# First slot of a fused attention and expert kernel: v's buffer 192 B longer, GpSimd's weight splits placed anew, routing with three small operations fewer, the ranks' product later on TensorE

## The chip, the cores and the metric

The kernel runs on one core of one Trainium2 chip. The metric is the time of one execution on the device in microseconds; less is better. The engines have short names in the profile: PE is TensorE (PEld its weight load), DVE is VectorE, ACT is ScalarE, POOL is GpSimd, SP is SyncE, which here only issues DMAs. A line such as L258 is a line of the kernel.

## The reference

Inputs are q, k and v for 8 batches, 8 heads, 576 tokens and head size 64, a modality id for each of the 4608 tokens, a gate, biases, eight experts' weights w1 (512x1024) and w2 (1024x512), and a last two-layer network with 512x2048 and 2048x512 weights.

```python
# linear attention: softmax of q over the head size, of k over the tokens
q_s = softmax(q, axis=-1); k_s = softmax(k, axis=2)
x = q_s @ (k_s^T @ v)                        # per batch and head, then [4608, 512]
# one expert for each token
logits = x @ w_gate + modality_bias[modality_id]
e_idx = argmax(logits)
gate_w = exp(l - max)[e_idx] / (sum(exp(l - max)) + 1e-9)
for e in range(8):
    mask = e_idx == e
    out[mask] = gate_w[mask] * (relu(x[mask] @ w1[e]) @ w2[e])
# last network
h = out @ w_in
result = max(0.01 * h, h) @ w_out
```

## The kernel before

The work stands in one program order, written out by hand, and each engine runs its own instructions in that order, waiting for what it needs.

**Attention** goes over four pairs of batches, i = 0 to 3. Each pair has nine chunks of 128 tokens, c = 0 to 8; (i, c) names a chunk here, and 9i + c is its place in time. The function `attention` makes a list of steps, each with a time in units of a chunk, and sorts it; the sorted list is the program order. For each chunk, `trans` transposes q on TensorE and ScalarE takes its exponent; `xmm` makes the product with the k-v matrix on TensorE and ScalarE copies the sums (ri) and the gate's logits (lr); `evac` on VectorE takes the reciprocal (L256), scales the product out of PSUM (L258), and SP stores it to xd. Two PSUM buffers hold the product of a chunk, so `xmm` of chunk n waits for `evac` of chunk n - 2. For the next pair, `kmax`, `kexp`, `kv`, `krec`, `kvn`, `kvT` and `kg` make the k-v matrix between them. `qmax` (VectorE, L219) and `qsub` (GpSimd, L223, 128x1536) take the maximum off q, a third of a pair at a time.

**Routing** (`phase_r`) is done for five groups of chunks: 0 to 8, 9 to 17, 18 to 26, 27 to 32 and 33 to 35; a route is named here by its first chunk. Its steps r0 to r16 are small VectorE instructions on all tokens of the group: logits, maximum, a one-hot choice oh, the counts of each expert (r8, tot), r9 (casts of the counts so far, tacc, and of tot to bf16, L326 and L327), r9t (tacc plus tot, L340), rm (the ranks' product on TensorE, with a triangle of ones, L332 to L336), r10 (the sum of exponents), r11 (plus 1e-9, L346), r12 to r15 (the row of every token, with a scan at L353) and r16 (that row as an integer, L362). Then `scat` on GpSimd writes each chunk's token numbers and weights to their rows of the table `region` by an indirect DMA (L365). A scatter may be `paced`: a copy of one element (L377) ahead of it waits for a given chunk's ri.

**The first slot.** Tokens are computed in slots of 512 of one expert. The first slot takes the expert with the most tokens of route 0, so that it can begin before the other routes are known. `First` chooses it. Its steps stand in the same list (`prepare`): `loads_to` loads chunks of w1 and w2 into a ring of five, `place1`, `place2` and `place3` reuse attention's k, v and q buffers for the split weights and operands, `idload` reads the tokens' numbers from `region` (SP, L624), `xids` casts them (L628), `xgather` fetches their rows of xd (GpSimd, four indirect DMAs, L633), `xgate1` scales them on ScalarE, and `xprep` transposes them. A float32 operand is split into a high part, rounded by a ScalarE cast (L510), and the rest, by a subtraction (L511) on VectorE or, where `eng` says so, GpSimd:

```python
def split(nc, hi, lo, src, eng=None):
    nc.scalar.copy(out=hi, in_=src)
    (eng or nc.vector).tensor_tensor(out=lo, in0=src, in1=hi.bitcast(F32), op=ALU.subtract)
```

`wsplit(s, which, c, eng, most)` does it for a quarter c of w1 or w2 of slot s. `slot0` is the first slot's first pass, x times w1: eight groups f of 12 matmuls (`pass1`, L659), each with a relu on ScalarE and a rest (`low`, L662) on VectorE. Steps of the sorted list that come after time 36.04 are run by `tail(f)` between its groups. `slot_tables` makes the table of all later slots there, in parts, with a small product on TensorE (L457). `slot0b` is the second pass, times w2 (`pass2`, L670), and gathers for slot 1. Then come the later slots (`slot`), up to 16 of them, with the same lines, the last network's weights being converted between their steps, and then the last network (`Hidden`, L934; `last_product`, L1093).

Of the kernel before, what the change touches and what calls it, by code (L numbers as in the profile page):

```python
# [99 lines left out]
def attention(ctx, pools, tc, cst, a, region, xd, first):  # L100
# [16 lines left out]
    tacc = cst["tacc"]  # L117
    kt, vt, qt = {}, {}, {}
    lr = one.tile([128, NPAIR * NC, 4, 16], F32, name="lr")
    ri = one.tile([128, NPAIR * NC, 4, 2], F32, name="ri")  # L120

    def load_kv(i, hp):
        if hp == 0:
            kt[i] = kp.tile([128, 4, 2 * S], F32, tag="k", name=f"k{i}")
            vt[i] = kp.tile([128, 4, 2, 5, 130], F32, tag="v", name=f"v{i}")
# [148 lines left out]
    def phase_r(c0, c1):  # L274
# [3 lines left out]
        t, rp = {}, {}  # L278

        def r0():  # L280
            t["lp"] = sp.tile([128, NC, 8, NE], F32, tag="lp", name="lp", bufs=1)[:, 0:n]
            for x in ("lg", "ex", "w"):
                t[x] = sp.tile([128, NC, NE], F32, tag=x, name=x)[:, 0:n]
# [5 lines left out]
            t["tot"] = sp.tile([128, NE], F32, tag="tot", name="tot")  # L289
            t["tb"] = sp.tile([128, 2, NE], BF16, tag="tb", name="tb")  # L290
# [19 lines left out]
        def rx():  # L310
            nc.scalar.activation(out=t["ex"], in_=t["lg"], func=AF.Exp)
# [10 lines left out]
        def r8():  # L322
            nc.vector.tensor_reduce(out=t["tot"], in_=t["oh"][:, :, 1:n + 1], axis=AX.X, op=ALU.add)

        def r9():
            nc.vector.tensor_copy(out=t["tb"][:, 1], in_=tacc)  # L326
            nc.vector.tensor_copy(out=t["tb"][:, 0], in_=t["tot"])  # L327

        def rm():
            bank = ps_k.tile([128, 3 * NE], F32, tag="kv", name="rp")  # L330
            rp[0] = bank[:, 0:NE]
            nc.tensor.matmul(bank[0:2 * NE, NE:2 * NE], lhsT=t["tb"].rearrange("p a e -> p (a e)"), rhs=trib[:, 0:NE], start=True, stop=True)  # L332
            nc.tensor.matmul(rp[0], lhsT=trib, rhs=t["tb"][:, 0], start=True, stop=False)
            nc.tensor.matmul(rp[0], lhsT=onesb, rhs=t["tb"][:, 1], start=False, stop=True)
            if c0 == 0:
                nc.tensor.matmul(bank[:, 2 * NE:3 * NE], lhsT=onesb, rhs=t["tb"][:, 0], start=True, stop=True)  # L336
                first.counts = bank[:, 2 * NE:3 * NE]

        def r9t():
            nc.vector.tensor_tensor(out=tacc, in0=tacc, in1=t["tot"], op=ALU.add)  # L340
# [3 lines left out]

        def r11():
            nc.vector.tensor_scalar(out=t["gs"], in0=t["gs"], scalar1=1e-9, scalar2=None, op0=ALU.add)  # L346
# [899 lines left out]
```

## Time and profile before

| what | value |
|---|---|
| runs | 1395.70, 1391.75 and 1393.58 us; median 1393.58 us |
| the profiled execution | 1389.55 us, of which the span of instructions is 1387.8 us |
| TensorE busy | 1319.7 us (95%), 9185 matmuls |
| VectorE, ScalarE, GpSimd busy | 1039.1, 584.5 and 333.2 us |
| granted TensorE clock, mean | 0.979 |

The runs are timings without a profile; all rows below are of the profiled execution, in us from the start of its span. TensorE's share is an average over stages: the attention stage ends at about 177 us, the first slot's passes go to about 235, the later slots to about 638 and the last network to the end.

### The profile page before, as it was taken

The page shows a single profiled execution, that of the slowest core. Times are in us where ns is not written, and L with a number is a line of the kernel's source. Part 1 is how long each engine was busy: PE and PEld are TensorE (multiplying, and loading weights), DVE is VectorE, ACT ScalarE, POOL GpSimd, SP SyncE. Part 2 cuts the span into 40 slices and gives each one's busy share as a digit, 9 for nine tenths or more (in the row PEclk, how much of TensorE's full clock was granted, in tenths as well). Part 3 has the DMA queues.
Part 4 walks back from the last instruction along what each step waited for, and adds up shares of the span by engine and source line. Part 5 has one row for each costly group of instructions (what it writes and reads, how often), then busy time and mean ns, then how long its engine had stood idle before and what let it go on. Part 6 is the DMA issues. An engine that isn't in the chain of part 4 may idle for free.

```text
span 1387.8 us, 23465 instructions
## 1 busy us (share of the span) xinstructions
PE 1319.7 (95%) x9185; PEld 1224.5 (88%) x9185; DVE 1039.1 (75%) x1398; ACT 584.5 (42%) x914; POOL 333.2 (24%) x285
## 2 busy tenths in 40 slices
PE   6997789999999999998999999999989999999998
PEld 6986667888878877888899999999979999999998
DVE  5789775778787777647678777778677877787775
ACT  4556424544555455454333233332233333333332
POOL 2227661111001100111343433333411110111011
PEclk9999799999999999999999999999999999999999
DMA  9874317779788887877823333323893434343430
GB/s 368 344 277 161 126 43 268 249 250 307 242 287 263 285 277 227 278 257 290 313 96 152 122 140 135 122 95 150 321 403 126 153 122 134 126 140 127 120 117 31
DMA packets 146444, 279.06 MB, mean 201 GB/s; under 512 B 18192, under 2 KB 69904, under 8 KB 145424
## 3 DMA queue, kind: packets, MB, share of 16 engines
q1 hardware_dynamic: 121536, 207.93, 44.4%
q10 hardware_dynamic: 17232, 48.48, 8.8%
q0 software_dynamic: 7552, 21.02, 4.4%
q8 instruction: 75, 1.23, 0.4%
q14 instruction: 49, 0.40, 0.1%
HBM read 181.07 MB, written 96.32 MB: 200 GB/s over the span
## 4 chain that ended last, share of the span: by engine, by line
PE 29%; DVE 11%; issue 7%; POOL 3%; DMA 2%; ACT 1%; POOLq 0%; SPq 0%; DVEq 0%; ACTq 0%
PE yp L1093 24%; PE hp L934 6%; POOL s L974 3%; DVE ht L947 2%; DVE ht L983 1%; DVE ht L980 1%; DVE s L971 1%; DVE ht L967 1%; DVE x L511 1%; DVE s L969 1%; POOL s L975 1%; DMA wi<-wid 1%; DMA hd<-ht 1%; DMA wo<-wod 1%; DVE xl L511 0%
## 5 line engine op out<-in xcount | busy, mean ns | idle before, releaser
L934 PE MATMUL hp<-xh,wi 128*128 128x256 f32 x1152 | 213.1, 281 | 4.7 <-DVE ht L983 2.3
L659 PE MATMUL hp<-xq,xk 128*128 128x512 f32 (+1 forms) x640 | 194.8, 388 | 0.9 <-issue 0.6
L1093 PE MATMUL yp<-wi,x 128*128 128x256 f32 x1152 | 191.4, 283 | 0.0
L934 PEld LDWEIGHTS hp<-xh,wi 128*128 128x128 f32 x1152 | 179.5, 188 | 7.5 <-DVE ht L983 3.5
L1093 PE MATMUL yp<-wi,wi 128*128 128x256 f32 x1200 | 178.2, 283 | 0.3 <-DVE wi L511 0.3
L934 PE MATMUL hp<-x,wi 128*128 128x256 f32 x1296 | 164.1, 286 | 5.5 <-ACTq L844 3.6
L934 PEld LDWEIGHTS hp<-x,wi 128*128 128x128 f32 x1296 | 160.5, 194 | 6.0 <-ACTq L844 3.8
L1093 PEld LDWEIGHTS yp<-wi,wi 128*128 128x128 f32 x1200 | 163.5, 192 | 0.6 <-DVE wi L511 0.6
L1093 PEld LDWEIGHTS yp<-wi,x 128*128 128x128 f32 x1152 | 161.9, 192 | 0.1
L934 PE MATMUL hp<-xl,wi 128*128 128x256 f32 x576 | 160.7, 279 | 0.0
L670 PE MATMUL yp<-xq,xk 128*128 128x512 f32 (+1 forms) x400 | 143.5, 388 | 0.6 <-DVE xq L662 0.6
L659 PEld LDWEIGHTS hp<-xq,xk 128*128 128x128 f32 x640 | 119.1, 190 | 27.8 <-issue 1.0
L633 POOL DMA_INDIRECT xg<-xd,idi x44 | 52.6, 1195 | 369.1 <-ACT xq L661 167.6
L511 DVE TENSOR_TENSOR xv<-st,xk 128x1024 fp32r<-128x1024 f32 x78 | 95.4, 1223 | 51.9 <-ACT xk L510 51.5
L659 PE MATMUL hp<-xq,xv 128*128 128x512 f32 (+1 forms) x320 | 123.7, 387 | 0.0
L670 PE MATMUL yp<-xq,xv 128*128 128x512 f32 (+1 forms) x320 | 123.1, 385 | 0.0
L1115 POOL DMA_INDIRECT out<-yo,idx x36 | 47.3, 1314 | 315.2 <-DVE idx L1109 294.3
L934 PEld LDWEIGHTS hp<-xl,wi 128*128 128x128 f32 x576 | 108.0, 187 | 0.0
L947 DVE SCALAR_TENSOR_TENSOR ht<-ht 128x1024 f32<-128x1024 f32 x72 | 104.9, 1457 | 2.5
L974 POOL TENSOR_TENSOR s<-s,s 128x512 f32<-128x512 f32 x36 | 48.6, 1351 | 211.0 <-DVE s L971 161.7
L510 ACT CAST xk<-st 128x1024 fp32r<-128x1024 f32 x84 | 87.6, 1044 | 13.9 <-ACT y L676 8.8
L661 ACT ACTIVATE xq<-hp 128x512 fp32r<-128x512 f32 (+1 forms) x80 | 46.1, 576 | 105.2 <-PE hp L659 100.2
(219 smaller groups left out, 2431.8 us busy)
## 6 DMA issues: line engine op xcount, KB each, us to landing
st<-in_w SPq DMA_DIRECT2D x88, 512.0 KB, 6.5
hd<-ht ACTq DMA_DIRECT2D x72, 512.0 KB, 3.0
xt<-hd SPq DMA_DIRECT2D x18, 1024.0 KB, 5.5
hr<-hd SPq DMA_DIRECT2D x18, 1024.0 KB, 5.3
wi<-wid SPq DMA_DIRECT2D x28, 512.0 KB, 9.2
wi<-wod SPq DMA_DIRECT2D x6, 2048.0 KB, 12.0
v<-in_v SPq DMA_DIRECT2D x16, 650.0 KB, 10.1
k<-in_k SPq DMA_DIRECT2D x16, 576.0 KB, 9.7
```

The lines of the kernel that those rows point to most:

```text
L510: nc.scalar.copy(out=hi, in_=src)
L511: (eng or nc.vector).tensor_tensor(out=lo, in0=src, in1=hi.bitcast(F32), op=ALU.subtract)
L633: nc.gpsimd.indirect_dma_start(out=xg[:, t], out_offset=None, in_=xd[0:n], in_offset=bass.IndirectOffsetOnAxis(ap=idis[s % 2][:, t:t + 1], ...
L659: nc.tensor.matmul(hp[:, rows], lhsT=w[:, k, 128 * f:128 * f + 128], rhs=x[:, k, rows], start=(n == 0), stop=(n == 11))
L661: nc.scalar.activation(out=hh[:, f, rows], in_=hp[:, rows], func=AF.Relu)
L670: nc.tensor.matmul(yp[:, rows], lhsT=w[:, f, 128 * d:128 * d + 128], rhs=h[:, rows], start=(n == 0), stop=(n == 23))
L934: self.nc.tensor.matmul(bank[:, g], lhsT=w[:, h, k, 128 * g:128 * g + 128], rhs=x[:, k], start=(n == 0), stop=(n == 5))
L947: V.scalar_tensor_tensor(out=c, in0=c, scalar=0.01, in1=c, op0=ALU.mult, op1=ALU.max)
L967: V.tensor_tensor(out=h[:, 0, 0], in0=bank, in1=s[1], op=ALU.add)
L974: G.tensor_tensor(out=s[6], in0=s[6], in1=s[5], op=ALU.add)
L1093: nc.tensor.matmul(bank, lhsT=x[:, k], rhs=w[i][:, h, k], start=(c == 0), stop=(c == 23))
L1115: ins = nc.gpsimd.indirect_dma_start(out=out, out_offset=bass.IndirectOffsetOnAxis(ap=idi[s % 2][:, t:t + 1], axis=0), in_=y[:, t], in_off ...
```

## The change

In the kernel after, v's buffer has 5248 elements of each partition in place of 5200, of which the first 5200 are used as before. Routing keeps the counts in one bf16 table `acc` with a place for each route, so that r9's two casts fall away: r8 writes its counts there, r9t adds them up there, and rm reads them there. The exponents have a ninth column that holds 1e-9, so that r10's sum has it and r11 falls away; r15 writes integers, so that r16 falls away. Scatters of routes 0, 9, 27 and 33 have other times, r12 to r15 of route 9 come later, and the ranks' products of routes 27 and 33 too have other times (the last one is run by `tail` of group 2 instead of group 1, that of 27 just ahead of the first pass). In `prepare`, the id load, the ids' cast and the gather come earlier, three of the four w1 splits are GpSimd's and come earlier, the fourth is VectorE's, and `xprep` is in two steps. In `slot0`, all four w2 splits are VectorE's, at other groups, the rests are computed later, and the tables are made at groups 2 and 3.

```diff
+VROW = 5248
...
+    acc, exs = cst["acc"], one.tile([128, 2, NC, NE + 1], F32, name="exs")
+    nc.gpsimd.memset(exs[:, :, :, NE], 1e-9)
...
     def load_kv(i, hp):
...
-            vt[i] = kp.tile([128, 4, 2, 5, 130], F32, tag="v", name=f"v{i}")
+            vt[i] = kp.tile([128, VROW], F32, tag="v", name=f"v{i}")[:, 0:5200].rearrange("p (h j c e) -> p h j c e", h=4, j=2, c=5)
...
+        tot, old, new = acc[:, u, 0], acc[:, u, 1], acc[:, u + 1, 1]
...
         def r0():
...
-            t["tot"] = sp.tile([128, NE], F32, tag="tot", name="tot")
-            t["tb"] = sp.tile([128, 2, NE], BF16, tag="tb", name="tb")
+            t["ex"] = exs[:, u % 2, 0:n]
...
         def rx():
-            nc.scalar.activation(out=t["ex"], in_=t["lg"], func=AF.Exp)
+            nc.scalar.activation(out=t["ex"][:, :, 0:NE], in_=t["lg"], func=AF.Exp)
...
         def r8():
-            nc.vector.tensor_reduce(out=t["tot"], in_=t["oh"][:, :, 1:n + 1], axis=AX.X, op=ALU.add)
-        def r9():
-            nc.vector.tensor_copy(out=t["tb"][:, 1], in_=tacc)
-            nc.vector.tensor_copy(out=t["tb"][:, 0], in_=t["tot"])
+                nc.vector.tensor_reduce(out=tot, in_=t["oh"][:, :, 1:n + 1], axis=AX.X, op=ALU.add)
...
         def rm():
...
-            nc.tensor.matmul(bank[0:2 * NE, NE:2 * NE], lhsT=t["tb"].rearrange("p a e -> p (a e)"), rhs=trib[:, 0:NE], start=True, stop=True)
-            nc.tensor.matmul(rp[0], lhsT=trib, rhs=t["tb"][:, 0], start=True, stop=False)
-            nc.tensor.matmul(rp[0], lhsT=onesb, rhs=t["tb"][:, 1], start=False, stop=True)
+            nc.tensor.matmul(bank[0:2 * NE, NE:2 * NE], lhsT=acc[:, u].rearrange("p a e -> p (a e)"), rhs=trib[:, 0:NE], start=True, stop=True)
+            nc.tensor.matmul(rp[0], lhsT=trib, rhs=tot, start=True, stop=False)
+            nc.tensor.matmul(rp[0], lhsT=onesb, rhs=old, start=False, stop=True)
...
-                nc.tensor.matmul(bank[:, 2 * NE:3 * NE], lhsT=onesb, rhs=t["tb"][:, 0], start=True, stop=True)
+                nc.tensor.matmul(bank[:, 2 * NE:3 * NE], lhsT=onesb, rhs=tot, start=True, stop=True)
...
         def r9t():
-            nc.vector.tensor_tensor(out=tacc, in0=tacc, in1=t["tot"], op=ALU.add)
+            nc.vector.tensor_tensor(out=new, in0=old, in1=tot, op=ALU.add)
...
         def r10():
...
-        def r11():
-            nc.vector.tensor_scalar(out=t["gs"], in0=t["gs"], scalar1=1e-9, scalar2=None, op0=ALU.add)
...
         def r15():
-            nc.vector.tensor_reduce(out=t["mx"], in_=t["st"][:, :, 0:n].rearrange("p e c -> p c e"), axis=AX.X, op=ALU.add)
-        def r16():
-            nc.vector.tensor_copy(out=t["ix"][:, 0:n], in_=t["mx"])
+                nc.vector.tensor_reduce(out=t["ix"][:, 0:n], in_=t["st"][:, :, 0:n].rearrange("p e c -> p c e"), axis=AX.X, op=ALU.add)
...
-    slow = dict(r0=1.15, r1=2.5, r2=3.5, rx=4.4, r5=4.5, r8=5.6, rm=6.55, r10=6.6, r12=7.6, r13=7.61, r16=8.5)
-    mid = dict(r0=0.2, r1=0.9, r2=1.2, rx=2.1, r5=2.15, r8=2.6, rm=3.3, r10=3.4, r12=4.1, r16=4.6)
-    fast = dict(r0=0.2, r2=0.6, rx=1.45, r5=1.15, rm=3.05)
-    route(0, 9, slow, 9.05, 0.7)
-    route(9, 18, slow, 9.2, 0.5)
+    slow = dict(r0=1.15, r1=2.5, r2=3.5, rx=4.4, r5=4.5, r8=5.6, rm=6.55, r10=6.6, r12=7.6, r13=7.61)
+    late9 = dict(slow, r8=5.3, rm=6.55, r10=6.6, r12=9.05, r13=9.06)
+    mid = dict(r0=0.2, r1=0.9, r2=1.2, rx=2.1, r5=2.15, r8=2.6, rm=3.3, r10=3.4, r12=4.1)
+    fast = dict(r0=0.2, r2=0.6, rx=1.45, r5=1.15, rm=2.95, r10=3.01)
+    route(0, 9, slow, 8.6, 0.55)
+    route(9, 18, late9, 9.4, 0.5)
...
-    route(27, 33, fast, 3.08)
-    route(33, 36, dict(r0=0.2, rm=1.2), 1.3)
+    route(27, 33, fast, 3.03)
+    route(33, 36, dict(r0=0.2, rm=2.1), 2.3)
...
-    tb = sp.tile([128, 2, NE], BF16, tag="tb", name="tb")[:, 0]
-    V.tensor_copy(out=tb, in_=cst["tacc"])
...
-    nc.tensor.matmul(np_, lhsT=cst["oneb"], rhs=tb, start=True, stop=True)
+    nc.tensor.matmul(np_, lhsT=cst["oneb"], rhs=cst["acc"][:, NROUTE, 1], start=True, stop=True)
...
-    yield
...
-    def xprep(k):
+    def xprep(k, wait=False):
...
-        split(nc, *(x[:, k].rearrange("d (p t) -> d t p", t=4) for x in (xh, xl)), tp)
+        hi, lo = (x[:, k].rearrange("d (p t) -> d t p", t=4) for x in (xh, xl))
+        nc.scalar.copy(out=hi, in_=tp)
+        low = lambda: nc.vector.tensor_tensor(out=lo, in0=tp, in1=hi.bitcast(F32), op=ALU.subtract)
+        if wait:
+            xlow[k] = low
+        else:
+            low()
...
     def prepare():
...
-        l += [(24.0, place1)] + [(24.1 + 0.6 * c, wsplit, 0, 1, c, G, 8) for c in range(4)]
-        l += [(25.0, idload, 0), (26.1, xids, 0), (26.6, xgather, 0), (28.0, place2)]
-        l += [(28.5 + 0.3 * t, xgate1, 0, t) for t in range(4)] + [(29.6 + k, xprep, k) for k in range(4)]
+        l += [(23.6, place1)] + [(23.65 + 0.7 * c, wsplit, 0, 1, c, G if c < 3 else None, 8) for c in range(4)]
+        l += [(23.5, idload, 0), (25.1, xids, 0), (25.6, xgather, 0), (28.0, place2)]
+        l += [(28.4 + 0.3 * t, xgate1, 0, t) for t in range(4)]
+        for k in range(4):
+            l += [(29.45 + k, xprep, k, True), (30.05 + k, lambda k=k: xlow.pop(k)())]
...
+        lows = []
         for f in range(8):
-            low = pass1(f, rows)
+            lows.append(pass1(f, rows))
             tail(f)
             if f == 1:
+                lows.pop(0)()
+                wsplit(0, 2, 0, None, 8)
+                wsplit(0, 2, 1, None, 8)
+                lows.pop(0)()
+            elif f == 2:
                 tables = slot_tables(tc, sp, ep, ps, cst, first, ti)
-            if tables:
+                next(tables)
+            elif f == 3:
+                lows.pop(0)()
+                next(tables)
+                lows.pop(0)()
                 next(tables, None)
-            low()
-            if 2 <= f < 6:
-                wsplit(0, 2, f - 2, G if f < 4 else None, 8)
-            if f == 5:
                 idload(1)
                 loads_to(11)
+            elif f == 5:
+                lows.pop(0)()
+                wsplit(0, 2, 2, None, 8)
+            elif f == 6:
+                lows.pop(0)()
+                wsplit(0, 2, 3, None, 8)
+        for low in lows:
+            low()
...
+        acc = con.tile([128, NROUTE + 1, 2, NE], BF16, name="acc")
+        nc.vector.memset(acc[:, 0, 1], 0.0)
+        cst["acc"] = acc
```

## Rows read from the trace of the kernel before

**Rows 1.** Windows: length, busy us of each engine, clock granted, DMA share, GB/s.
```profile
120.00:140.00 20.00, 10.19 (x84) 9.54 (x84) 18.96 (x27) 11.55 (x30) 17.44 (x14) 0.88 0.31 104
140.00:160.00 20.00, 14.50 (x87) 12.95 (x88) 14.68 (x27) 8.88 (x24) 13.82 (x17) 0.76 0.52 172
160.00:180.00 20.00, 14.72 (x92) 12.39 (x92) 16.60 (x44) 7.71 (x21) 14.85 (x23) 0.85 0.24 82
180.00:206.78 26.78, 23.63 (x95) 18.39 (x93) 20.98 (x66) 8.12 (x13) 15.73 (x14) 0.87 0.07 12
300.00:400.00 100.00, 100.00 (x450) 81.45 (x449) 76.77 (x95) 53.14 (x65) 9.60 (x8) 1.00 0.79 253
```

**Rows 2.** Timeline of TensorE, first slot: start, length, instruction, [idle before and its releaser].
```profile
177.59 0.72 PE L659 MATMUL hp<-xq,xk 128*128 128x512 f32 x2 [0.34 <-DVE xr L258]
...
187.24 0.19 PE L457 MATMUL np<-tb,trib 128*128 128x8 bf16 x1 [1.94 <-DVE tb L455]
...
206.78 0.39 PE L670 MATMUL yp<-xq,xk 128*128 128x512 f32 x1
```

**Rows 3.** Timeline of VectorE, end of attention's third pair.
```profile
126.62 2.22 DVE L326 CAST tb<-tacc 128x8 bf16<-128x8 f32 x1
...
130.47 8.96 DVE L346 TENSOR_SCALAR gs<-gs 128x9 f32<-128x9 f32 x1
...
142.19 2.90 DVE L353 TENSOR_TENSOR_SCAN st<-cf,oh 128x80 f32<-128x80 f32 x1
```

**Rows 4.** Groups by line, VectorE, 0 to 260: busy us, mean ns, idle before.
```profile
L327 DVE CAST tb<-tot 128x8 bf16<-128x8 f32 x5 | 0.8, 164 | 0.0
```

**Rows 5.** Timeline of GpSimd, 126 to 163.
```profile
126.06 2.76 POOL L223 TENSOR_TENSOR q<-q,qm 128x1536 f32<-128x1536 f32 x1 [0.82 <-DVE ri L256]
...
130.15 9.24 POOL L511 TENSOR_TENSOR xv<-st,xk 128x1024 fp32r<-128x1024 f32 x4
...
147.03 1.04 POOL L633 DMA_INDIRECT xg<-xd,idi  x1 [2.11 <-DVE ri L256]
...
160.00 2.77 POOL L223 TENSOR_TENSOR q<-q,qm 128x1536 f32<-128x1536 f32 x1
```

**Rows 6.** Timeline of TensorE, 130 to 144.
```profile
130.19 1.24 PE L244 MATMUL xp<-kvx,eq 128*128 128x146 f32 x8 [0.42 <-DVE rk L170]
131.26 0.60 PE L185 MATMUL tp<-cf,kvx 128*128 128x128 f32 x4
...
140.48 3.24 PE L249 MATMUL xp<-kvx,eq 128*64 128x146 f32 x16 [8.18 <-DVE xr L258]
```

**Rows 7.** Timeline of VectorE, attention's last pair.
```profile
159.07 1.08 DVE L511 TENSOR_TENSOR xq<-tp,xq 128x512 fp32r<-128x512 f32 x1 [4.27 <-ACT xq L510]
...
160.21 2.60 DVE L326 CAST tb<-tacc 128x8 bf16<-128x8 f32 x1
...
165.36 1.09 DVE L511 TENSOR_TENSOR xq<-tp,xq 128x512 fp32r<-128x512 f32 x1 [1.14 <-ACT xq L510]
```

**Rows 8.** Windows of the first pass.
```profile
187.30:192.50 5.20, 5.20 (x13) 4.10 (x14) 2.36 (x14) 0.00 (x0) 3.98 (x5) 0.50 0.02 1
193.50:206.70 13.20, 13.20 (x58) 10.70 (x57) 12.99 (x22) 6.03 (x8) 5.96 (x3) 1.00 0.03 4
```

**Rows 9.** Timeline of VectorE, first pass.
```profile
194.85 2.54 DVE L488 TENSOR_TENSOR ek<-ek 128x256 f32<-128x256 f32 x1
...
197.52 2.37 DVE L493 TENSOR_TENSOR ek<-ek 128x8 f32<-128x8 f32 x1
...
203.82 1.22 DVE L511 TENSOR_TENSOR xv<-st,xk 128x1024 fp32r<-128x1024 f32 x1
```

**Rows 10.** Timeline of ScalarE, first cast of a w1 split.
```profile
127.80 1.04 ACT L510 CAST xk<-st 128x1024 fp32r<-128x1024 f32 x1
```

**Rows 11.** Costliest groups of the page: busy us, mean ns, idle before.
```profile
L659 PE MATMUL hp<-xq,xk 128*128 128x512 f32 (+1 forms) x640 | 194.8, 388 | 0.9 <-issue 0.6
...
L659 PE MATMUL hp<-xq,xv 128*128 128x512 f32 (+1 forms) x320 | 123.7, 387 | 0.0
```

More of the change, by code (lines that the diff above doesn't have):

```diff
@@ L28 @@
 NSTATIC = 9
+NROUTE = 5
 MT = 256
+VROW = 5248
 LASTC = 6
@@ L116, in attention @@
         kvx.append(t)
-    tacc = cst["tacc"]
+    acc, exs = cst["acc"], one.tile([128, 2, NC, NE + 1], F32, name="exs")
+    nc.gpsimd.memset(exs[:, :, :, NE], 1e-9)
     kt, vt, qt = {}, {}, {}
+    nroute = [0]
     lr = one.tile([128, NPAIR * NC, 4, 16], F32, name="lr")
@@ L278, in phase_r @@
         t, rp = {}, {}
+        u = nroute[0]
+        nroute[0] += 1
+        tot, old, new = acc[:, u, 0], acc[:, u, 1], acc[:, u + 1, 1]
         def r0():
             t["lp"] = sp.tile([128, NC, 8, NE], F32, tag="lp", name="lp", bufs=1)[:, 0:n]
-            for x in ("lg", "ex", "w"):
+            for x in ("lg", "w"):
                 t[x] = sp.tile([128, NC, NE], F32, tag=x, name=x)[:, 0:n]
@@ L322, in r8 @@
         def r8():
-            nc.vector.tensor_reduce(out=t["tot"], in_=t["oh"][:, :, 1:n + 1], axis=AX.X, op=ALU.add)
-        def r9():
-            nc.vector.tensor_copy(out=t["tb"][:, 1], in_=tacc)
-            nc.vector.tensor_copy(out=t["tb"][:, 0], in_=t["tot"])
+            with nc.allow_low_precision("whole numbers up to 36"):
+                nc.vector.tensor_reduce(out=tot, in_=t["oh"][:, :, 1:n + 1], axis=AX.X, op=ALU.add)
         def rm():
@@ L358, in r15 @@
         def r15():
-            nc.vector.tensor_reduce(out=t["mx"], in_=t["st"][:, :, 0:n].rearrange("p e c -> p c e"), axis=AX.X, op=ALU.add)
-        def r16():
-            nc.vector.tensor_copy(out=t["ix"][:, 0:n], in_=t["mx"])
+            with nc.allow_low_precision("whole numbers"):
+                nc.vector.tensor_reduce(out=t["ix"][:, 0:n], in_=t["st"][:, :, 0:n].rearrange("p e c -> p c e"), axis=AX.X, op=ALU.add)
         def scat(c):
@@ L369, in scat @@
             tc.add_to_no_dep_group("scatter", ins.ins)
-        return dict(r0=r0, r1=r1, r2=r2, r3=r3, r4=r4, rx=rx, r5=r5, r6=r6, r7=r7, r8=r8, r9=r9, r9t=r9t, rm=rm, r10=r10,
-                    r11=r11, r12=r12, r13=r13, r14=r14, r15=r15, r16=r16), [(scat, c) for c in range(n)]
+        return dict(r0=r0, r1=r1, r2=r2, r3=r3, r4=r4, rx=rx, r5=r5, r6=r6, r7=r7, r8=r8, r9t=r9t, rm=rm, r10=r10,
+                    r12=r12, r13=r13, r14=r14, r15=r15), [(scat, c) for c in range(n)]
     pace = one.tile([1, 1], F32, name="pace")
@@ L646, in xgate @@
             xgate1(s, t)
-    def xprep(k):
+    xlow = {}
+    def xprep(k, wait=False):
         tp = ps2.tile([128, 4, 128], F32, tag="t", name="tp")
@@ L1176, in build @@
         cst["biasT"] = biasT
-        tacc = con.tile([128, NE], F32, name="tacc")
-        nc.vector.memset(tacc, 0.0)
-        cst["tacc"] = tacc
+        acc = con.tile([128, NROUTE + 1, 2, NE], BF16, name="acc")
+        nc.vector.memset(acc[:, 0, 1], 0.0)
+        cst["acc"] = acc
         z = acon.tile([128, (NE * NT + SLOT) // 64], F32, name="z")
```

## The prediction, made before the kernel after had run

> **What bounds the kernel now.** I read first the table of windows, to find where TensorE is not full [rows 1]: the reader is to see that it works 10.19 of 20 us from 120 on, 14.50 and 14.72 of 20 in the two windows behind, 23.63 of 26.78 up to 206.78, and 100.00 of 100 later. That is 23.7 us of idle time between 120 and 206.78, at the end of attention and in the first slot's first pass. From 206.78, where that slot's second pass begins [rows 2], TensorE is the bound, and all later work is tied to it by program order. So what the change is worth is how much earlier that second pass begins.
>
> Second I read the timelines of the engines in this stretch, each to see one thing. VectorE [rows 3]: a 128x8 cast (r9) stands 2.22 us from 126.62, and a 128x9 add (r11) 8.96 us from 130.47, where a small cast takes 0.16 with nothing in its way [rows 4]. GpSimd [rows 5]: over the first lies the q subtraction of 126.06 (2.76 long, so to 128.82), over the second four weight splits back to back (130.15, 9.24 together, to 139.39). VectorE's small instruction waits until GpSimd's are through. TensorE [rows 6]: it waits 8.18 us for the evacuation that is queued behind r11. VectorE later [rows 7]: 4.27 and 1.14 us of waiting for ScalarE's casts of the gathered x, since the gather began only at 147.03 [rows 5], and a 2.60 us r9 under the subtraction of 160.00. First pass [rows 2, 8]: it begins at 177.59; at 187.24 TensorE has waited 1.94 for the table's cast, and then runs at a granted clock of 0.50 (the 1.2 GHz level) until 192.5, against 1.00 (2.4 GHz) behind.
>
> **Stall one, 126 to 140 us.** The change takes r9 and r11 away. But r9t stays, at r9's place in VectorE's order, right behind r8, and it has two inputs in SBUF. Such an instruction is blocked by GpSimd too: L488, a tensor_tensor, stands 2.54 us and L493, 128x8, 2.37 us, each under one of GpSimd's splits [rows 9]. So r9t takes over r9's stall from about 126.6. What lies behind the subtraction on GpSimd is new: the scatters are done earlier and three splits follow at once. Their first cast ended at 128.84 in the kernel before [rows 10] and stands earlier in ScalarE's order now, so GpSimd need not wait. Two rows bound what r9t does at 128.82. It may get through there, as r9 did ahead of a scatter; or it waits through the whole row of splits, as r11 did through four, past three boundaries [rows 3, 5]. Splits behind one another are what r9t meets, so I take the second: blocked to 128.82 + 3 x 2.31 = 135.75, released 3.6 us before r11 was (139.4). The work queued behind is larger: evacuation (2,5) has not gone, so TensorE still owes product (2,7) and the transposes for kvT and q, 1.24 + 0.60 + 0.60 = 2.4 us at the high clock (the second transpose group is taken like the first) and up to 4.9 at half [rows 6]. Gain between 3.6 - 2.4 = +1.2 and 3.6 - 4.9 = -1.3; I take +0.2, nearer to the high clock's end only by a little, as the 8.18 us pause was followed by slow products (3.24 us for sixteen at 140.48).
>
> The Trainium skill (SBUF — State Buffer, "Who interferes with whom") says that whichever of the two engines issues first has the shared pair of ports for that whole instruction, and that the other blocks; by that, r9t would wait for one instruction and no more. The 8.96 us of r11 [rows 3] do not fit one split of 2.31. What the rule would give stands among the rivals.
>
> **The moved split, ids and gather.** The fourth split goes to VectorE: 1.22 us [rows 9], while TensorE has its last products, kvT and kg, for which VectorE waits there; taken as nothing, 1.2 if that cover is gone. The id load now stands ahead of the splits on SP, behind nine scatters that are paced closer and earlier; xids stands ahead of a long maximum, and the four gathers ahead of the next q subtraction. In the kernel before, the gather began 7.6 us after r11's release, with that maximum, a scan of 2.90 under a subtraction [rows 3] and the subtraction itself between. So it now begins between 135.8 and 143.4; I take 138.5, since of all that only evacuations are left. Even 143.4 is 3.6 earlier than 147.03. VectorE's two waits of 4.27 and 1.14 go [rows 7]: 5.4 us, 3.6 at least. Queued behind the gathers is the q subtraction; its chunks are used some 2.8 us after the gathers' end or later, so it costs nothing, 1 at worst. r12 to r15 of route 9 move behind two evacuations; their scan will meet the later subtraction again: no gain and no loss, since TensorE's kg covers both.
>
> r9t of route 18 has r9's place there, and its 2.60 us [rows 7] either stay or go: the subtraction (160.00 before) now comes at about the same moment as r9t. Between 0 and 2.4 I take 1.2. Some six small casts and adds fewer on VectorE from there to the first pass, at a little under 0.1 each (164 ns is one with its latency, the starts are closer) [rows 4]: 0.5. VectorE sets TensorE's pace in this stretch (16.60 of 20 busy [rows 1], and the rest are the waits named), so these count in full. The first pass begins 0.2 + 5.4 + 1.2 + 0.5 = 7.3 us earlier.
>
> **The first slot's first pass.** Before: 177.59 to 206.78, 29.2 us [rows 2]. The steady pace is 13.2 us for 57 matmuls [rows 8], 0.232 each, so 96 take 22.3. The ranks' product of the last route and the table's product now come behind the third of eight groups, when their inputs have long been made; with them 22.7. That gains 6.5: the waits (1.94 at 187.24 the longest), the half clock that follows, and the small products. VectorE takes two more w2 splits (2 x 1.22), but the tables no longer stand under GpSimd's (2.54 and 2.37, some 4.3 of it waiting [rows 9]); with 20.98 busy before [rows 1] it has about 19 to do in 22.7, and the second pass asks for the last pieces only when three quarters of its first group are through. Against this, the next slot's id load hangs on the tables; they were done when the split of 203.82 began [rows 9], 3.0 us ahead of the second pass, and by my count of VectorE's order will be done some 2 us ahead. I take off 1 us for a later gather in slot 1, from 0 to 3.
>
> v's 192 bytes and the other table of exponents: nothing. The first pass's matmuls take 388 ns with their weights in one buffer and 387 in the other [rows 11], whatever their addresses.
>
> **Sum.** 7.3 + 6.5 - 1.0 = 12.8 us. The profiled execution took 1389.55, so 1376.8; the median of the runs shown is 1393.58, 4 us above it, so 1380.8.
>
> **Rivals.** (A) The forecast: 1380.8, its own range 1378 to 1384.
>
> (B) r9t gets through at 128.82. For it: r9 did [rows 3, 5]. Against: r11 did not at three boundaries. Then (2,7), kvT and the rest run while the splits go on. At the outside the whole 6.9 us of splits are won; r12 to r15 and the scan under the later subtraction (2.90) then come into the path. So 4 to 6 us more than A: 1380.8 - 5 = 1375.8. By the rule of the Trainium skill (SBUF — State Buffer, "Who interferes with whom") the time would be this one.
>
> (C) Part is lost to VectorE: r9t of route 18 keeps its stall (1.2 of the sum), the split on VectorE is not covered (1.2), and a w2 split or two reach the second pass late (1.22 each). With about 4.2 lost: 1385.
>
> (D) The earlier start is hidden: slot 1's ids, gather or weight loads do not come earlier, and TensorE waits for them in the second pass instead. The shrinking margin of the id load speaks for it; against it, all of them are issued by order, not by time, and the memory is far from busy up to 206.78 (DMA share 0.07 [rows 1]). 1391.
>
> (E) Slower: the shifted addresses. All slots read weights and operands in the moved buffers; the first passes have 640 + 320 matmuls [rows 11] and the second passes as many, at 0.232 some 445 us of a full TensorE. Each 1% costs 4.5 us: from 2.9% it eats the 12.8, from 3.8% (0.232 to 0.241 us) the kernel is slower by more than 0.3%: 1398 or more. Against it: rows 11.
>
> **Numbers.** Chances: A 0.43, B 0.22, C 0.20, D 0.09, E 0.06. 0.3% is 4.2 us, about what a measurement of this kernel can tell from no change. A, B and C are faster by more: 0.85; D is the same: 0.09; E slower: 0.06. The range, from B's middle less 2 to C's far end, is 1374 to 1388.5 and leaves out B's tail, D and E.
>
> **What would show it.** Right: on VectorE no r11, but one long instruction, r9t, at 126.6 that ends with the third split, near 135.7 (B: near 128.8); gathers from about 138; no waits for the casts of x; the first pass near 170 and 22.7 long at a granted clock of 1.00; the second pass near 193. Wrong: a long instruction of VectorE elsewhere under the splits (the cast of the ids is a candidate), a first pass that waits for VectorE, new idle time of TensorE behind the second pass's start, or matmuls that no longer pace at 0.232.

## The result, and the profile after

The kernel after takes 1362.96 us (median of 4 runs, 1361.30 to 1363.15) where the kernel before took 1393.28 us beside it (4 runs): a ratio of 0.978, 95% interval 0.976 to 0.980. That is 30 us faster. The forecast was 12.8 us, and the time lies outside the range given. The profiled execution after took 1363.15 us, its span 1361.4.

The windows of the kernel after, cut at the first pass's start and end, answer to [rows 1]:

```profile
120.00:140.00 20.00, 18.32 (x140) 17.04 (x138) 18.41 (x36) 14.80 (x41) 16.50 (x12) 0.91 0.61 193
140.00:160.00 20.00, 14.59 (x91) 13.52 (x90) 15.65 (x31) 11.18 (x25) 18.23 (x25) 0.83 0.33 119
160.00:169.20 9.20, 3.92 (x25) 3.19 (x23) 4.14 (x14) 1.57 (x7) 5.89 (x11) 0.68 0.14 44
169.20:191.95 22.75, 22.75 (x102) 18.54 (x103) 18.57 (x64) 8.34 (x15) 11.55 (x12) 0.98 0.10 20
300.00:400.00 100.00, 99.19 (x458) 82.17 (x458) 80.10 (x97) 53.03 (x65) 9.63 (x8) 1.00 0.88 283
```

The reader sees two things. TensorE works 18.32 of the 20 us from 120 on (10.19 before [rows 1]), and the first pass is full: it begins at 169.2 (177.59 before [rows 2]) and the second pass at 191.95 (206.78). That is 14.8 us, about the 7.3 + 6.5 of the forecast. And in the later slots, where TensorE was full before too, it now does 458 matmuls in 100 us in place of 450. This second gain the forecast did not have. The last network began 638.13 us into the span before and 616.00 after, so 7.3 of the 22.1 us came behind the first slot's first pass. The rest, to the last matmul, went from 744.4 to 740.2 us.

The page's groups of the kernel after, which answer to [rows 11]:

```profile
L663 PE MATMUL hp<-xq,xk 128*128 128x512 f32 (+1 forms) x640 | 189.8, 380 | 0.7 <-issue 0.7
...
L663 PE MATMUL hp<-xq,xv 128*128 128x512 f32 (+1 forms) x320 | 121.1, 379 | 0.0
```

One matmul of the first passes fell from 388 and 387 to 380 and 379 ns, in both weight buffers alike (from start to start, in a later slot, 233.3 and 226.7). No instruction was changed there.

VectorE and GpSimd of the kernel after, near 125, answer to [rows 3, 5]:

```profile
125.11 1.75 DVE L343 TENSOR_TENSOR acc<-acc 128x8 bf16<-128x8 bf16 x1
...
129.19 2.32 DVE L624 CAST idi<-idt 128x4 int32<-128x4 f32 x1
```

```profile
124.08 2.76 POOL L227 TENSOR_TENSOR q<-q,qm 128x1536 f32<-128x1536 f32 x1 [1.78 <-issue]
126.81 6.99 POOL L507 TENSOR_TENSOR xv<-st,xk 128x1024 fp32r<-128x1024 f32 x3
133.96 1.84 POOL L629 DMA_INDIRECT xg<-xd,idi  x1 [0.16 <-issue]
```

r9t (L343) gets through when the subtraction ends at 126.84, ahead of the three splits, and not behind them at 133.8: rival B. The gather begins at 133.96 (147.03 before).

Chunk (2,8), which before waited until 140.48 [rows 6], and the last two chunks of attention, on TensorE; then ScalarE's exponent for the last one:

```profile
130.66 1.77 PE L253 MATMUL xp<-kvx,eq 128*64 128x146 f32 x16
...
159.40 1.16 PE L248 MATMUL xp<-kvx,eq 128*128 128x146 f32 x8
165.84 3.24 PE L253 MATMUL xp<-kvx,eq 128*64 128x146 f32 x16 [5.28 <-ACT eq L240]
```

```profile
165.19 0.60 ACT L240 ACTIVATE eq<-tq 128x512 f32<-128x512 f32 x1 [3.99 <-remote]
```

Chunk (3,7), at 159.40, stood at 172.34 before:

```profile
172.34 1.27 PE L244 MATMUL xp<-kvx,eq 128*128 128x146 f32 x8 [0.31 <-DVE xr L258]
```

So TensorE is 12.9 us ahead there, and 8.4 at the first pass: the last chunk waited 5.28 us for ScalarE, which itself stood 3.99 us. "Remote" says that the trace doesn't hold what released it.

### The profile page after: what moved, and what is told of

The parts are those of the page before. It is cut to its first block, busy times and chain, and to the rows that moved or that the text cites. A ratio compares the mean times of both kernels' runs of the same rounds, so it can differ in the third digit from the quotient of the medians.

```text
span 1361.4 us, 23447 instructions
## 1 busy us (share of the span) xinstructions
PE 1300.6 (96%) x9185; PEld 1216.1 (89%) x9185; DVE 1023.2 (75%) x1380; ACT 585.1 (43%) x914; POOL 328.1 (24%) x283
## 3 DMA queue, kind: packets, MB, share of 16 engines
q8 instruction: 75, 1.23, 0.4%
## 4 chain that ended last, share of the span: by engine, by line
issue 29%; DVE 11%; POOL 7%; PE 3%; DMA 3%; ACT 1%; POOLq 0%; SPq 0%; DVEq 0%; ACTq 0%
POOL out L1135 3%; PE hp L954 3%; POOL s L994 3%; DVE ht L967 2%; DMA hd<-ht 2%; DVE ht L1000 1%; DVE s L991 1%; DVE ht L1003 1%; DVE ht L987 1%; DVE s L989 1%; DVE x L507 1%; POOL s L995 1%; DMA wi<-wid 1%; DVE xl L507 0%; ACT ht L996 0%
## 5 line engine op out<-in xcount | busy, mean ns | idle before, releaser
L663 PE MATMUL hp<-xq,xk 128*128 128x512 f32 (+1 forms) x640 | 189.8, 380 | 0.7 <-issue 0.7
L1113 PE MATMUL yp<-wi,x 128*128 128x256 f32 x1152 | 188.5, 280 | 0.6 <-DVE x L507 0.6
L1113 PE MATMUL yp<-wi,wi 128*128 128x256 f32 x1200 | 174.5, 280 | 0.4 <-DVE wi L507 0.4
L1113 PEld LDWEIGHTS yp<-wi,wi 128*128 128x128 f32 x1200 | 160.1, 188 | 0.6 <-DVE wi L507 0.6
L1113 PEld LDWEIGHTS yp<-wi,x 128*128 128x128 f32 x1152 | 158.7, 189 | 0.8 <-DVE x L507 0.8
L507 DVE TENSOR_TENSOR xv<-st,xk 128x1024 fp32r<-128x1024 f32 x81 | 99.6, 1231 | 50.9 <-ACT xk L506 46.6
L506 ACT CAST xk<-st 128x1024 fp32r<-128x1024 f32 x84 | 87.7, 1047 | 14.3 <-ACT y L680 8.7
L996 ACT ACTIVATE ht<-s 128x512 f32<-128x512 f32 x36 | 22.8, 634 | 152.5 <-POOL s L995 147.4
```

What stands on the lines that cost most here:

```text
L663: nc.tensor.matmul(hp[:, rows], lhsT=w[:, k, 128 * f:128 * f + 128], rhs=x[:, k, rows], start=(n == 0), stop=(n == 11))
L996: nc.scalar.activation(out=h[:, 1, 1], in_=s[5], func=AF.Relu)
L1113: nc.tensor.matmul(bank, lhsT=x[:, k], rhs=w[i][:, h, k], start=(c == 0), stop=(c == 23))
```

## The experiments

The built program gives each buffer's byte offset on a partition. Before, the slots' weights lie at 49504 (k, w1's high part), 86368 and 107168 (v, the low parts) and the moving operands at 127968 (q). After, they lie at 49664, 86528, 107520 and 128512: the bf16 table ahead of them is 160 bytes longer than tacc was, and v's first buffer 192. "Distance" below is the moving operand's offset less that of its weights, modulo 256. From k and from v's first buffer to q it was 128 bytes before and is 0 after; from v's second buffer, 64 and 0. A slot's time is counted from the start of its first pass to that of the next.

**Order against addresses.** Four kernels, made in pairs from before and after:

```diff
 x1_con32 (before)
-        tacc = con.tile([128, NE], F32, name="tacc")
+        tacc = con.tile([128, 2 * NE], F32, name="tacc")[:, 0:NE]
 x2_vrow (before)
-            vt[i] = kp.tile([128, 4, 2, 5, 130], F32, tag="v", name=f"v{i}")
+            vt[i] = kp.tile([128, 5248], F32, tag="v", name=f"v{i}")[:, 0:5200].rearrange(...)
 x4_addr (before): as x2_vrow, and tacc [128, 48]
 x3_sched (after): VROW = 5200, acc [128, NROUTE + 4, 2, NE]
```

> The kernel before with one table (tacc) 32 bytes longer on each partition and nothing else, so that every later buffer of SBUF lies 32 bytes further on: the buffers k, q, st and wi1 then begin at a multiple of 128 bytes (before: 96 above one), v's two at 0 and 64 above one. Theory 'addresses': the last 12 us of the gain come from where the slots' operands lie. Then rows of 128x512 in the slots go at 0.226 to 0.227 us in place of 0.231, the stretch from the first slot's second pass to the last network is 7 us shorter, the last product 4 to 5 us shorter, the first pass still begins near 177.6 and the whole takes 1380 to 1383 us. Rival 'schedule': the pace comes from other things of the change (what VectorE and the DMA queues do at the time); then 1393 us, no change.

> The kernel before with v's buffer 5248 elements long and nothing else. All buffers keep their place within 128 bytes but for v's second one (still 32 above a multiple of 64). Theory 'addresses' in the form that the place within 64 or 128 bytes counts: no change, 1392 to 1394 us. Theory 'v's length': the 192 bytes alone bring the faster pace, 1381 us.

> The kernel after with its new table 96 elements of 2 bytes longer in all (by three unused places) and v's buffer 5200 long again, so that every buffer of the slots lies within 128 bytes as in the kernel before. What is left is the change of order alone. Theory 'addresses': rows of 128x512 go at 0.231 us again, the first pass begins near 169 and the second near 192 to 193, and the whole takes 1376 to 1380 us. Rival 'schedule': 1363 us as the kernel after.

> The kernel before with the table 192 bytes long and v's buffer 5248 long, so that every buffer lies at exactly the address that it has in the kernel after. Theory 'addresses': 1379 to 1383 us, with 0.226 to 0.227 us a row of 128x512 in the slots. If it is the same as with 32 bytes alone, v's length is worth nothing; if it is better by some us, the second v buffer (0 against 64 above a multiple of 128) counts too. Rival 'schedule': 1393 us.

Measured, beside 1392.93 us for the kernel before: x1 1389.11 (ratio 0.998, 0.997 to 1.000), x2 1387.00 (0.996, 0.995 to 0.997), x4 1380.49 (0.991, 0.989 to 0.994), x3 1374.94 (0.988, 0.985 to 0.990). So order alone gives 18.0 us and addresses alone 12.4, by the medians, together the whole 30. But the forms "multiple of 128" and "v's place within 64" both fell: x1, with every buffer but v's second at a multiple of 128, kept a slow slot (46.29 us, as before), and x2, which keeps each place but v's second, made it fast (45.33). x1 instead made the last product faster (741.0 us from the last network's start to the last matmul, 744.4 before), which x2 did not (745.7). The same window of x1 and then of x2:

```profile
300.00:400.00 100.00, 100.00 (x449) 81.40 (x449) 77.72 (x94) 51.52 (x64) 9.61 (x8) 1.00 0.81 267
```

```profile
300.00:400.00 100.00, 99.83 (x457) 82.65 (x455) 78.60 (x96) 54.31 (x67) 9.60 (x8) 1.00 0.82 261
```

What x2 and x4 have in common, and x1 and x3 lack, is the distance: v's length moves q by 384 bytes against k. So v's 192 bytes are worth the 5.9 us of x2. The other 6.5 us of x4 came with the longer count table, which moves buffers of the last network: the last product took 360.0 us in x4, 366.3 in x2.

**The distance by itself.** m1_offsets runs rows of 96 matmuls alone.

```python
def seq(w, x, n):   # weights at w and 4096 elements behind, moving operand at x
...
for m in seq(0, 8192, 512): T.matmul(**m)    # distance 0
for m in seq(0, 8200, 512): T.matmul(**m)    # distance 32
```

> A kernel that leaves out the whole computation and measures the disputed cost by itself: rows of 96 matmuls in the order of a slot's first pass, all operands in one buffer, each row on a line of its own. Scan 1: 512 columns, the distance from weights to moving operand (modulo 512 bytes) goes from 0 to 480 in steps of 32, nothing else runs. Scan 2: both operands moved by 32, 64 or 96 bytes, at distances 0 and 128. Scan 3: as scan 1 with 256 columns. Scan 4: distances 0 and 128, while VectorE writes 128x1024 subtractions to 0, 32, 64 or 96 above a multiple of 128. Theory 'distance': what counts is how far the moving operand lies from the weights; in the runs so far the slots were fast (0.2245 to 0.227 us) where it is 0 and slow (0.231 to 0.232) where it is 128 or 320. Then scan 1 gives 0.225 at 0 and 0.232 at 128 and 320, scan 2 nothing for the place as such, scan 4 the same two paces wherever VectorE writes. Rival 'place': scan 1 and 2 differ by the operand's own place within 64 or 128 bytes. Rival 'writes': scans 1 to 3 are flat near 0.225, and only scan 4 has slow rows, those where VectorE writes at 32 or 64.

Windows of it, one row each: 512 columns at 0, 32, 64 and 128 bytes, then 256 columns at 0, 32, 128 and 192:

```profile
66.08:87.84 21.76, 21.76 (x97) 18.02 (x96) 0.16 (x1) 0.00 (x0) 0.00 (x0) 1.00 0.00 1
87.84:110.25 22.41, 22.41 (x98) 18.00 (x97) 0.16 (x1) 0.00 (x0) 0.00 (x0) 1.00 0.00 1
110.25:132.23 21.98, 21.98 (x97) 18.03 (x96) 0.16 (x1) 0.00 (x0) 0.00 (x0) 1.00 0.00 1
154.64:177.04 22.40, 22.40 (x97) 18.02 (x96) 0.16 (x1) 0.00 (x0) 0.00 (x0) 1.00 0.00 1
555.11:566.62 11.51, 11.51 (x97) 11.51 (x96) 0.16 (x1) 0.00 (x0) 0.00 (x0) 1.00 0.01 1
566.62:577.93 11.31, 11.31 (x98) 11.31 (x97) 0.16 (x1) 0.00 (x0) 0.00 (x0) 1.00 0.00 0
...
600.75:612.14 11.39, 11.39 (x98) 11.39 (x97) 0.16 (x1) 0.00 (x0) 0.00 (x0) 1.00 0.01 1
623.41:634.32 10.91, 10.91 (x99) 10.91 (x97) 0.16 (x1) 0.00 (x0) 0.00 (x0) 1.00 0.01 2
```

Each row's time over 96, in ns, by distance; 256 to 480 gave the same again within 0.2:

```
distance       0     32     64     96    128    160    192    224
512 columns  226.7  233.4  229.0  233.4  233.3  234.2  233.2  233.2
256 columns  119.9  117.8  117.8  119.9  118.6  117.4  113.6  118.2
```

Both operands moved together by 32, 64 or 96 bytes gave 227.1 at 0 and 233.2 at 128, and VectorE's writing changed nothing, wherever it wrote (226.7 to 227.2 and 233.2 to 233.3). So "distance" holds; "place" and "writes" fall. The slots went at the very paces of the table: 233.3 ns a matmul in the first passes before, 226.7 after. That the table repeats at 256 was not expected. It explains the last product too: most of its pairs went from 0 to 32 bytes in x1, 119.9 to 117.8 ns, and to 160 in x4 and in the kernel after, 117.4.

m2_fine asked two things more.

> As the first measuring kernel (the computation is left out, rows of 96 matmuls alone), with two questions. First, distances between the steps of 32 bytes: if the pace hangs on 32-byte pieces, a distance of 4 to 16 bytes already goes at the 0.233 us that 32 had; if it changes smoothly, 4 and 8 bytes stay near the 0.2267 us of distance 0, and with 256 columns the best is near 192 bytes, perhaps below 0.1136 us. Second, which weights count: rows whose weights lie in turn at 0 and 128 bytes, so that a moving operand is at one distance from its own weights and at another from the next one's, which are loaded while it streams. Theory 'next': 512 columns go at 0.233 us with 0 to its own and 128 to the next, and at 0.2267 the other way about; 256 columns at 0.1185 with 192 to its own and 64 to the next and at 0.1136 the other way about. Rival 'own': both the other way. If the two are alike, both count or neither does.

With 512 columns, 4 bytes went at 237.5 ns and 16 at 231.8, so the pace hangs neither on 32-byte pieces nor smoothly on the distance. With weights in turn at 0 and 128 bytes, 0 to its own and 128 to the next gave 228.4 and the reverse 230.1; with 256 columns both ways gave 116.7. Neither theory: both distances count.

**The distance in the kernel, without v.** z1_gap_q moves q alone:

```diff
+            if i == 0:
+                kp.tile([128, 32], F32, tag="gap", name="gap", bufs=1)
```

> The kernel before with an unused 128 bytes ahead of the q buffers and nothing else: v keeps its 5200 elements, and no buffer but q's moves. From the slots' weights to the moving operands it is then 0 in place of 128 bytes (modulo 256) in the first passes; in the second passes the pairs with w2's low part (v's second buffer) go from 64 to 192, the others from 128 to 0. Theory 'distance', by the rows measured alone: the first passes go at 0.225 to 0.227 us a row of 512 columns, the second ones little faster than before, a slot takes 45.5 us in place of 46.3, the stretch from the first slot's second pass to the last network 426 us in place of 431.4, the whole 1386 to 1389 us. Rival 'v's length' (or v's own place): 1393 us.

It took 1385.61 us beside 1389.55 (0.996, 0.995 to 0.997). A slot took 45.73 us. The first passes went at 0.2268 us a matmul, as the table gives; the second ones, 23.96 us long, no faster than before (23.89). (The loaded weights' ring moved 128 bytes as well; it is no operand of a matmul.) The stretch to the last network shrank only to 429.8 us in its profiled execution, whose first slot's second pass took 30.4 us (27.6 before). v's length is not needed: "distance" holds in the kernel, for the first passes.

**The order, part by part.** e1_fold takes r11 away alone; e2_slot0 takes over `slot0` and the late ranks' products alone; e4_acc_slot0 is e2 with the counts in bf16 as well:

```diff
 e1_fold (before)
+            t["ex"] = exs[:, u % 2, 0:n]          # ninth column 1e-9
-        def r11():
 e2_slot0 (before): slot0 of after; fast rm=2.95, r10=3.01; route(33, 36, dict(r0=0.2, rm=2.1), 2.3)
 e4_acc_slot0 (before): as e2_slot0, and acc with r8, r9t, rm, r15 and slot_tables of after
```

> The kernel before with r11 alone taken away (1e-9 stands in a ninth column of the exponents); r9's casts, r16, all splits and times stay. By the forecast's step 'stall one', another small instruction waits through the splits in r11's place, and it is worth 0.2 us: 1393 us. By rival B, a small instruction gets through at the next boundary of GpSimd's work, and the 8.96 us of r11 were its own bad luck or kind: TensorE's wait of 8.18 us goes, of which later stalls give some back, 1386 to 1390 us.

> The kernel before with the change's order of the first slot's first pass alone (all w2 splits on VectorE, rests later, tables at groups 2 and 3, the last ranks' product at group 2, that of route 27 just ahead). By the forecast: that pass takes 22.7 us in place of 29.2 to 31, 1 us of it is lost to slot 1's later gather, 1386 to 1388 us. Rival 'hidden': slot 1's gather and weights don't come earlier, and TensorE waits for them in the second pass: 1391 us or more.

> The kernel before with two parts of the change: the counts in a bf16 table (r9's casts, r16 and the tables' cast fall away) and the order of the first slot's first pass; r11 and all that stands ahead of that pass stay, and all buffers keep their place modulo 256. That order alone had left a first pass of 26.5 us, in which TensorE waited 3.32 us for VectorE ahead of the tables' product, whose input is cast behind two w2 splits. Theory 'cast': without that cast the product's input is long there, the first pass takes 22.8 to 23.5 us, and the whole is 5 to 8 us below the kernel before. Rival 'VectorE late': the wait stays in another place, 2 to 3 us below the kernel before as with the order alone.

e1 took 1384.83 and e2 1387.47 beside 1389.55 (0.996, 0.995 to 0.998, and 0.999, 0.997 to 1.000); e4 took 1385.13 beside 1393.58 (0.994, 0.992 to 0.996). By the medians e1 is worth 4.7 us, a little more than rival B had, though not by its mechanism, as the next part shows. e2 is worth only 2.1, hardly clear of nothing: its first pass took 26.5 us, and TensorE waited in it, as its timeline shows:

```profile
191.11 0.18 PE L457 MATMUL np<-tb,trib 128*128 128x8 bf16 x1 [3.32 <-DVE ek L462]
```

VectorE's timeline says why. The table's cast stands behind two splits that the new order put ahead of it:

```profile
186.36 2.38 DVE L510 TENSOR_TENSOR xv<-st,xk 128x1024 fp32r<-128x1024 f32 x2 [1.51 <-ACT xk L509]
...
190.70 0.33 DVE L455 CAST tb<-tacc 128x8 bf16<-128x8 f32 x1
```

e4, which needs no cast, has no such wait, a first pass of 23.3 us, and gains 8.5 us. "Cast" holds: the order pays only with the bf16 table. (r9's casts and r16 went with it; the cast alone was not tried.) e1 and e4 give 13.2 of the 18.0 us. The other 4.8, by subtraction and only if the parts add up, are the moved split, ids, gather and scatters, which were not tried alone.

**Who waits through the splits.** In e1 the stall did not vanish. It went to the next instruction that met the splits, as the forecast's step said, the scan, which waited through the last three of them (to 138.45) and the q subtraction behind (to 141.20):

```profile
132.27 9.12 DVE L355 TENSOR_TENSOR_SCAN st<-cf,oh 128x80 f32<-128x80 f32 x1
```

The gain came from the order behind it: the evacuations no longer stood behind the stall, and the product of chunk (2,8) began at 131.28 (140.48 before). Then TensorE waited 5.83 us at 143.11.

e3_r11 (after, with r11 put back), e5_four (e3 with the fourth split on GpSimd) and e6_three (e4 with the fourth on VectorE) looked for what decides it.

```diff
 e3_r11 (after)
+        def r11():
+            nc.vector.tensor_scalar(out=t["gs"], in0=t["gs"], scalar1=1e-9, scalar2=None, op0=ALU.add)
 e5_four (e3_r11): G for all four c;   e6_three (e4_acc_slot0): G if c < 3 else None
```

> The kernel after with r11 put back behind r10 (the ninth column holds 0), so that it starts in the middle of GpSimd's first of three splits, near 128.2. Theory 'row': a small instruction with its input and output in SBUF that starts under a row of splits waits through all of them, as r11 and, in its place, the scan did: until 133.8, 3 to 5 us more than the kernel after. Theory 'boundary': it gets through at the next one, 129.1, as the cast of the ids did in the kernel after: 0 to 1.5 us more.

> The kernel after with r11 put back (as before) and with the fourth w1 split on GpSimd again, so that four stand in a row there. Theory 'number': r11 now waits through all four, some 9 us, as in the kernel before. Rival 'other': it gets through at the first boundary in under 2.4 us, as with three.

> The kernel before with the counts in bf16 and the first pass's new order (r11 waited 9.15 us there, through four splits), and the fourth w1 split now on VectorE, so that three stand in a row. Theory 'number': r11 gets through at the first boundary, in under 2.4 us. Rival 'other': it waits through all three, 6 to 7 us.

e3 took 1364.31 us (0.979 of before, 0.977 to 0.981), e5 1360.76 and e6 1384.80 in one run each. r11 in e3, in e4, and then in e6 with GpSimd's row behind it:

```profile
129.22 0.90 DVE L349 TENSOR_SCALAR gs<-gs 128x9 f32<-128x9 f32 x1
```

```profile
129.40 9.15 DVE L349 TENSOR_SCALAR gs<-gs 128x9 f32<-128x9 f32 x1
```

```profile
130.07 6.85 DVE L349 TENSOR_SCALAR gs<-gs 128x9 f32<-128x9 f32 x1
```

```profile
129.93 6.95 POOL L510 TENSOR_TENSOR xv<-st,xk 128x1024 fp32r<-128x1024 f32 x3
```

In e3 (splits from 127.72) it got through at the first boundary, in e6 behind all three, with the same three splits. So "number" falls, and e5 could not decide it: there the gathers came between the third split and the fourth. In all that starved (before, e1, e4, e6) the splits followed a scatter; in all that got through (after, e3, e5) they followed the q subtraction at once. e5 shows both in one kernel: r11 got through ahead, and an addition that met the fourth split, right behind a gather, waited through it and the q subtraction behind:

```profile
138.96 5.21 DVE L308 TENSOR_TENSOR lg<-lg,biasT 128x72 f32<-128x72 f32 x1
```

```profile
139.00 2.35 POOL L510 TENSOR_TENSOR xv<-st,xk 128x1024 fp32r<-128x1024 f32 x1
141.30 2.77 POOL L227 TENSOR_TENSOR q<-q,qm 128x1536 f32<-128x1536 f32 x1
```

Scatters and gathers are both indirect DMAs that GpSimd issues, so an indirect DMA right ahead of the row goes with starving in each of these cases. r11 also stood 0.1 to 0.3 us behind the splits' start where it starved and 1.5 where not. That alone doesn't decide: the cast of the ids in the kernel after stood 0.06 us behind a split's start and got through. No run changed what stands ahead of the row and nothing else, so the cause stays open.

**A version beyond both.** In the last network the distances after were 0, 64, 96, 160 and 224. b1_dist192 makes all of them 192:

```diff
-        self.w1 = p.tile([128, 21, 1024], F32R, name="wi1")
+        self.w1 = p.tile([128, 21536], F32R, name="wi1")[:, 8:21512].rearrange("p (n x) -> p n x", n=21)
...
-        ring.append((half(w0[:, 4]), half(w0[:, 5])))
+        r0, r3 = ([half(t[:, a + 1024 * n:a + 1024 * n + 1024]) for n in range(3)] for t, a in ((hidden.w0f, 4112), (hidden.x3f, 32)))
+        ring.append((r0[0], r0[1]))
```

b2_dist112 has 4132 and 52 there, 112 bytes in the last product. m3_order runs the two orders of matmuls alone, with 256 columns.

> The kernel after with the last network's buffers moved, so that every matmul of 256 columns there has 192 bytes (modulo 256) from its weights and the next ones to the moving operand (in the kernel after it is 0, 64, 96, 160 or 224); the slots keep their 0. Theory 'distance', by the rows measured alone: 256 columns go at 0.1136 us in place of 0.117 to 0.120, some 5700 matmuls by 3 to 6 ns: 20 to 28 us less than the kernel after, 1335 to 1343 us. Rival: TensorE isn't alone there, and VectorE, ScalarE or the loads of weights keep the pace: less than 10 us, 1353 us or more. Rival 'place': no change, 1363 us.

> The computation is left out; rows of 96 matmuls of 256 columns alone, in the order of the last product (for each k the high weights twice, then the low ones) and in that of the hidden layer, at distances 0 to 252 bytes. Theory 'order': at 192 bytes the hidden layer's order goes at 0.113 us and the last product's at 0.1175, and by changing the step of the weights, the place of the low ones or the step of the moving operand one finds which of them counts. Rival 'company': both orders go at 0.1136 at 192 alone, and in the kernel other engines or DMAs hold the last product.

> As the version with 192 bytes everywhere in the last network, but with 112 bytes from weights to moving operand in the last product. Theory 'state': the slow pace belongs to 192 bytes, and at 112 the last product goes at 0.1133 us in place of 0.1177: some 2800 matmuls by 4 ns, 11 us less than with 192, near 1345 us. Rival 'company': something that runs beside the last product holds it at 0.1175 to 0.118 us whatever the distance; no change against 192, near 1356 us.

b1 took 1355.83 us (1350.72 to 1362.40, 6 runs; 0.973, 0.970 to 0.976, against 0.976 to 0.980 for the kernel after): better by some 7 us, with intervals that touch, not by 20 to 28. In its profiled execution (1359.82 us) the last network took only 1.3 us less than after. In the hidden layer the pace came (113 ns) and waits took it back, as its group in b1 shows:

```profile
L956 PE MATMUL hp<-xh,wi 128*128 128x256 f32 x1152 | 205.9, 278 | 15.9 <-ACT s L983 13.1 <-DVE ht L1005 2.8
```

After, that group had 3.7 us of idle time ahead of it; the hidden layer took 378.3 us in place of 379.3. In the last product the pace stayed at 117.5 to 117.9 ns. Alone, both orders went at 113.5 to 113.6 at 192 bytes, but two rows of m3 that stood first went at 117.7 and 117.8, with the same operands: this distance has two paces. At 112 bytes (113.3 alone) the last product went at 116.7 in b2, which took 1361.03 us (1350.00 to 1364.36; 0.980, 0.978 to 0.982), no better than the kernel after. The hidden layer of b2, still at 192 bytes, shows both paces of 192, some blocks of its loop at 117.8 ns and some at 113.3, switching only where TensorE had paused. Two windows of 24 us, one of each:

```profile
706.00:730.00 24.00, 24.00 (x206) 24.00 (x205) 20.57 (x24) 7.73 (x14) 10.34 (x9) 1.00 0.28 111
750.00:774.00 24.00, 24.00 (x214) 24.00 (x213) 20.66 (x27) 8.06 (x15) 8.86 (x7) 1.00 0.33 132
```

The other engines are about as busy in both, so "company" isn't needed for the 117.8 ns of b1's last product; "state" fits it. b1's six times also lie in two groups, 1350.7 to 1351.8 and 1359.8 to 1362.4 us, about what some 2800 matmuls at the one pace or the other differ by (12 us). But only an execution of the upper group was profiled, so that this is the reason is not shown. What chooses the pace, and why 112 bytes gave 116.7, is open.

## Why the prediction was wrong, step by step

- **"v's 192 bytes and the other table of exponents: nothing"** is the step that failed: 12.4 us (x4_addr). [Rows 11] were read as two buffers at different addresses with one pace. They are at one distance, 128 bytes, from the operand that both meet, so they could not show what a distance does. v's 192 bytes made that distance 0 (5.9 us, x2). The shift by the longer count table was not costed at all (the other 6.5). Rival E had the right quantity, TensorE's pace in all slots, with the wrong sign: the first passes went from 0.2333 to 0.2267 us a matmul, 3%, and the stretch of the last network from 744.4 to 740.2 us.
- **Stall one, +0.2.** This failed too, by the wait. Rival B held: r9t waited for one GpSimd instruction, 1.75 us. At chunk (2,8) TensorE was 9.8 us ahead, 1.6 of it from before 127 us. The Trainium skill (SBUF — State Buffer, "Who interferes with whom") says that whoever issues first has the shared pair for the whole instruction and the other blocks. r9t's wait agrees; the 9.12, 9.15 and 6.85 us of e1, e4 and e6 are longer than any one instruction of GpSimd there.
- **The first pass begins 7.3 us earlier.** It was 8.4 in the kernel after and 9.7 in x3_sched's trace, but that it came so near is luck. Stall one gave some 8 us in place of 0.2, and the last chunk of attention gave 4.5 of the lead back, in a wait that the forecast did not have (5.28 us). e5 and b2, with nearly the same order, wait 2.4 and 2.0 us there, and their first pass begins 12.4 and 14.3 us earlier than before. VectorE's waits for the gathered x shrank from 4.27 and 1.14 to 1.23 and 0.16 us.
- **First pass 29.2 to 22.7 us, +6.5.** Right in length (22.8). The working named the cover but not its condition: without the bf16 table the same order leaves 26.5 us (e2).
- **A later gather in slot 1, −1.0.** The first slot's second pass took 27.6 us before, 27.1 after and 28.1 in x3_sched, and 26.0 (b2) to 30.7 (e3) in others with after's order. No loss of 1 us can be told from that.
- **The sum.** By x3_sched's trace the order gave 15.2 us of span where 12.8 were forecast; timed it gave 18.0, and its 1374.94 us lie in the range, near rival B's 1375.8. The profiled execution before lies 3.4 us under the median of 1392.93: its first slot, both passes, took 56.8 us, and 57.7 to 59.5 in five kernels with the same order there (x1, x2, x4, z1, e1).

## What to carry to other kernels

A change of a tile's size moves every buffer behind it. Where TensorE is full, work out the distance from weights to moving operand, modulo 256 bytes, for each pair before and after, and look up or measure its price; two rows show that addresses cost nothing only if this distance differs between them. An order of work that is copied without the cheaper instruction it relies on may bring a quarter of its gain, so undo parts in pairs too.

## What the runs showed of the hardware that was not expected

TensorE's pace at full clock (1.00 granted, the 2.4 GHz level) hangs on the distance between its two operands in SBUF, modulo 256 bytes: 226.6 to 237.5 ns for 512 columns and 113.3 to 121.7 for 256, with no other engine at work. Of those tried, the best distance is 0 for 512 columns, and 192 or 112 for 256, where 192 has two paces, 113.3 to 113.6 and 117.8 ns. Why is not shown. The Trainium skill (SBUF — State Buffer, "Who interferes with whom") calls TensorE's two reads independent; these rows differ, and the measurement decides. And a VectorE instruction that takes 0.2 to 0.3 us elsewhere may starve behind two to four GpSimd instructions, past the boundaries between them (5.21 to 9.15 us).
